# Laying a two-layer kernel's inputs out on the host: direct loads, two more resident weight units, no PE transposes

## The chip, the cores and the metric

The kernel runs on one core of a Trainium2 chip. The metric is the device time of one execution in microseconds, taken as the median of several. Engine names are those of the profile: PE is the matmul engine, PEld its weight load, DVE the vector engine, ACT the scalar engine, POOL is GpSimd, SP the engine that only issues transfers. A name with a q (SPq) is that engine's sequencer. On one core the spread of a kernel is about plus or minus 0.3%. A difference under 2% is called "same" here, even where it is clear of noise. A profile is one execution, so its times scatter as much.

## The reference, cut to what matters

```python
x = x + A(layernorm(x))      # A: memory-augmented recurrent attention, 64 segments of 32 rows
x = x + B(layernorm(x))      # B: sliding, dilated attention, window 8
x = x + A(layernorm(x))      # the same weights again
x = x + B(layernorm(x))
# A, per segment: h = [mem (8 rows), segment (32 rows)]; q,k,v = h Wq, h Wk, h Wv; attention;
# o = . Wo; mem = o[:8] goes into the next segment.  D = 640, 32 heads of 192
```

The memory makes layer A sequential: 64 segments one after the other. The weights of A are 31.5 MB, of which only a part stays on the chip.

## The kernel before

Both passes run at once, as two "lanes" of 40 columns: pass 2 follows pass 1 at a lag of three segments. So 67 steps of A carry 80 columns each, and 69 steps in all finish B. A's weights are cut into 32 units of 0.983 MB. 14 stay in SBUF ("resident"), 18 are loaded again in every step into a ring of four buffers. The sources lie in DRAM in rows of 1280 or 1536 bytes, so that the first load of each ring unit is followed by a copy back to DRAM in rows of 7680 bytes, from which all later steps load.

```python
def unit(self, kind, i):
    ...
    if res:  t_ = self.wres.tile([P, 3840], BF16, ...)
    else:    t_ = self.wring.tile([P, 3840], BF16, name="w_ring")
    if (kind, i) in self.wcopy: nc.sync.dma_start(out=t_[:], in_=self.wcopy[(kind, i)][:])
    else:                       nc.sync.dma_start(out=v, in_=src)          # short rows
    ...
    elif (kind, i) not in self.wcopy:                                      # ring unit, step 0
        self.wcopy[(kind, i)] = self.dram.tile([P, 3840], BF16, ...)
        nc.gpsimd.dma_start(out=self.wcopy[(kind, i)][:], in_=t_[:])
...
def proj_stationary(self, kind, i, t):        # k and q: 30 matmuls of 80 columns
    ...
    nc.tensor.matmul(ps[:, NT*n:NT*(n+1)], lhsT=w[:, c, P*n:P*(n+1)], rhs=hT[:, NT*c:NT*(c+1)], ...)
...
def x_transpose(self, g):                     # every fourth step; y_store likewise
    for c in range(NC):
        nc.tensor.transpose(out=ps[:, c, :], in_=xr[:, P*c:P*(c+1)], identity=self.ident[:])
    nc.scalar.copy(out=xt[:], in_=ps[:])
```

Layer B's weights (wqkv, wo) are loaded at the very start on ACT's queue.

Of the kernel before, what the change touches and what calls it, by code (L numbers as in the profile page):

```python
# [16 lines left out]
DRAM = bass.MemoryType.DRAM  # L17
# [23 lines left out]
N_RES = 14  # L41
# [20 lines left out]
class Kernel:  # L62
    def __init__(self, ctx, tc, A_x, A_mem0, A_Wq, A_Wk, A_Wv, A_Wo, B_wqkv, B_wo, out):
        self.tc = tc
        self.nc = tc.nc
        self.x = A_x[0]
        self.mem0 = A_mem0[0]
        self.out = out[0]
        self.n_seg = A_x.shape[1] // SEG
        self.wsrc = {"k": A_Wk.rearrange("d h e -> d (h e)"), "q": A_Wq.rearrange("d h e -> d (h e)"),  # L70
                     "v": A_Wv.rearrange("d h e -> d (h e)"), "o": A_Wo.rearrange("h e d -> (h e) d")}
        pool = lambda name, bufs, **kw: ctx.enter_context(tc.tile_pool(name=name, bufs=bufs, **kw))
        self.cp = pool("consts", 1)
        self.wres = pool("wres", 1)
        self.wring = pool("wring", RING)
        self.ap2 = pool("act2", 2)
        self.bp = pool("bact", 1)
        self.xp = pool("xio", 1)
        self.ps_big = pool("ps_big", 4, space=PSUM)
        self.ps_one = pool("ps_one", 1, space=PSUM)  # L80
        self.units = {}
        self.wcopy = {}
        self.dram = pool("wdram", 1, space=DRAM)
        self.resident = resident_units()
        self.build_consts(B_wqkv, B_wo)

    def build_consts(self, B_wqkv, B_wo):
        nc, cp = self.nc, self.cp
        nc.scalar.preload_act_table_set("natural_log_exp_and_others")
        ident = cp.tile([P, P], BF16, name="ident")  # L90
        make_identity(nc, ident[:])
        self.ident = ident
# [5 lines left out]
        self.ones = ones  # L98

# [10 lines left out]
        self.maskA = mA  # L110

# [31 lines left out]
        def pers(name, shape, n, dt=BF16, zero=True):  # L143
            ts = []
            for j in range(n):
                t_ = cp.tile(shape, dt, name=f"{name}{j}")
                if zero:
                    nc.vector.memset(t_[:], 0.0)
                ts.append(t_)
            return ts  # L150

        self.hT = pers("hT", [P, NC * NT + 88], 2)
        self.KF = pers("KF", [P, 4 * NT + 48], 2)
        self.Kz = pers("Kz", [P, 4 * NT + 48], 2)
        self.Vt = pers("Vt", [P, 1152], 2)
        self.xin = pers("xin", [P, NC, NX], 3)
        self.h2T = pers("h2T", [P, NC, P], 1)[0]
        self.KB = pers("KB", [P, NBC, P], 1)[0]
        self.VB = pers("VB", [P, BH // 2, 2 * BD + 1], 1)[0]
        nc.vector.memset(self.VB[:, :, BD:BD + 1], 1.0)  # L160
        self.On = pers("On", [P, 3 * P], 1)[0]
        self.YT = pers("YT", [P, NC, P], 1, zero=False)[0]
        self.m0T = pers("m0T", [P, NC, NM], 1, zero=False)[0]
        self.wqkv = cp.tile([P, NC, 3 * D], BF16, name="wqkv_sb")
        nc.scalar.dma_start(out=self.wqkv[:], in_=B_wqkv.rearrange("(c p) n -> p c n", p=P))
        self.wo = cp.tile([P, 2, 3, D], BF16, name="wo_sb")
        nc.vector.memset(self.wo[64:P, :, 2, :], 0.0)
        for par in range(2):
            r0 = par * (D // 2)
            nc.scalar.dma_start(out=self.wo[:, par, 0:2, :], in_=B_wo[r0:r0 + 2 * P, :].rearrange("(m p) n -> p m n", p=P))  # L170
            nc.scalar.dma_start(out=self.wo[0:64, par, 2, :], in_=B_wo[r0 + 2 * P:r0 + D // 2, :])

    def unit(self, kind, i):
        if (kind, i) in self.units:
            return self.units[(kind, i)]
        nc = self.nc
        res = (kind, i) in self.resident
        if kind == "o":
            src = self.wsrc["o"][QE * i:QE * (i + 1), :].rearrange("(m p) d -> p m d", p=P)
        else:  # L180
            src = self.wsrc[kind][:, QE * i:QE * (i + 1)].rearrange("(c p) n -> p c n", p=P)
        if res:
            t_ = self.wres.tile([P, 3840], BF16, name=f"w_{kind}{i}")
        else:
            t_ = self.wring.tile([P, 3840], BF16, name="w_ring")
        v = t_[:].rearrange("p (a b) -> p a b", a=6 if kind == "o" else NC)
        if (kind, i) in self.wcopy:
            nc.sync.dma_start(out=t_[:], in_=self.wcopy[(kind, i)][:])
        else:
            nc.sync.dma_start(out=v, in_=src)  # L190
        if res:
            self.units[(kind, i)] = v
        elif (kind, i) not in self.wcopy:
            self.wcopy[(kind, i)] = self.dram.tile([P, 3840], BF16, name=f"wc_{kind}{i}")
            nc.gpsimd.dma_start(out=self.wcopy[(kind, i)][:], in_=t_[:])
# [7 lines left out]

    def proj_stationary(self, kind, i, t):
# [3 lines left out]
        ps = self.big(f"ps_{kind}")  # L208
        for n in range(6):
            for c in range(NC):  # L210
                nc.tensor.matmul(ps[:, NT * n:NT * (n + 1)], lhsT=w[:, c, P * n:P * (n + 1)], rhs=hT[:, NT * c:NT * (c + 1)],  # L211
# [3 lines left out]
    def a_k(self, i, t):  # L215
# [5 lines left out]
        nc.scalar.copy(out=kf, in_=pv[:, :, 0:3:2, :])  # L221
        nc.scalar.copy(out=kz[0:64, :, 0, :], in_=pv[0:64, :, 1, :])
        nc.scalar.copy(out=kz[64:P, :, 1, :], in_=pv[64:P, :, 1, :])

    def a_q(self, i, t):
        ps = self.proj_stationary("q", i, t)
        qt = self.ap2.tile([P, 6, NT], BF16, name="QT")
        self.nc.vector.tensor_copy(out=qt[:], in_=ps[:, 0:6 * NT].rearrange("p (a n) -> p a n", a=6))  # L228
# [19 lines left out]
    def a_s(self, i):  # L248
# [3 lines left out]
        kf, kz, qt = self.KF[i % 2], self.Kz[i % 2], self.qt  # L252
        for h in range(4):
            pr, j = h // 2, h % 2
            nc.tensor.matmul(sv[:, h, :], lhsT=kf[:, NT * h:NT * h + P], rhs=qt[:, 3 * pr + 2 * j, :], start=True, stop=False)  # L255
            nc.tensor.matmul(sv[:, h, :], lhsT=kz[:, NT * h:NT * h + P], rhs=qt[:, 3 * pr + 1, :], start=False, stop=True)  # L256
        e = self.ap2.tile([P, 4, NT], BF16, name="E")
        nc.scalar.activation(out=e[0:NT], in_=sv[0:NT], func=ACT.Exp, scale=float(DH) ** -0.5)  # L258
        em = self.ap2.tile([P, 4, NT], BF16, name="Em")
        nc.vector.tensor_tensor(out=em[0:NT], in0=e[0:NT], in1=self.maskA[0:NT, :].unsqueeze(1).to_broadcast([NT, 4, NT]), op=ALU.mult)  # L260
        self.em = em

    def a_pv(self, i):
# [3 lines left out]
        dn = self.one("d")  # L267
        nc.tensor.matmul(dn[:, 0:4 * NT], lhsT=self.ones[0:NT, :], rhs=em[0:NT, :, :].rearrange("p h n -> p (h n)"), start=True, stop=True)  # L268
        ops = self.one("o")
        ov = ops[:, 0:6 * NT].rearrange("p (a b n) -> p a b n", a=2, b=3)  # L270
        for pr in range(2):
            for (b, w0, j, st, sp) in [(0, 0, 0, True, True), (1, 128, 0, True, False), (1, 256, 1, False, True), (2, 384, 1, True, True)]:
                nc.tensor.matmul(ov[:, pr, b, :], lhsT=vt[0:NT, 512 * pr + w0:512 * pr + w0 + P], rhs=em[0:NT, 2 * pr + j, :], start=st, stop=sp)  # L273
        r = self.ap2.tile([P, 2, 2, NT], F32, name="R")
        rf = r[:].rearrange("p a b n -> p (a b n)")
        nc.scalar.activation(out=rf, in_=dn[:, 0:4 * NT], func=ACT.Ln)  # L276
        nc.scalar.activation(out=rf, in_=rf, func=ACT.Exp, scale=-1.0)  # L277
        ot = self.ap2.tile([P, 2, 3, NT], BF16, name="OT")
        nc.vector.tensor_tensor(out=ot[:, :, 0:3:2, :], in0=ov[:, :, 0:3:2, :], in1=r[:], op=ALU.mult)  # L279
        nc.vector.tensor_tensor(out=ot[0:64, :, 1, :], in0=ov[0:64, :, 1, :], in1=r[0:64, :, 0, :], op=ALU.mult)  # L280
        nc.vector.tensor_tensor(out=ot[64:P, :, 1, :], in0=ov[64:P, :, 1, :], in1=r[64:P, :, 1, :], op=ALU.mult)
        self.ots[i] = ot

    def a_o(self, i):
# [5 lines left out]
        for m in range(6):  # L290
            for c in range(NC):
                nc.tensor.matmul(self.acc[:, NT * c:NT * (c + 1)], lhsT=w[:, m, P * c:P * (c + 1)], rhs=ot[:, m, :],  # L292
# [5 lines left out]
    def mem_out(self, t):  # L298
# [6 lines left out]
        else:  # L305
            nc.vector.tensor_copy(out=h[:, :, :, 0:NM], in_=a[:, :, :, 0:NM])
# [35 lines left out]
    def b_x1(self, b):  # L342
        nc = self.nc
        a = self.lanes(self.acc[:, 0:NC * NT])
        x1 = self.x1p.tile([P, NC, NX], BF16, name="x1")
        nc.vector.tensor_tensor(out=x1[:].rearrange("p c (l n) -> p c l n", l=2), in0=a[:, :, :, NM:LT],
                                in1=self.xin[b % 3][:].rearrange("p c (l n) -> p c l n", l=2), op=ALU.add)
        self.x1[b] = x1
        self.bsq = self.ln_sq(x1)

    def b_ln(self, b):
        self.bmr = self.ln_small(self.ln_stats(self.x1[b], self.bsq))

    def b_ln_apply(self, b):
        self.ln_big(self.x1[b], self.bmr, self.h2T[:, :, 64 * (b % 2):64 * (b % 2) + NX].rearrange("p c (l n) -> p c l n", l=2))
# [91 lines left out]
    def b_wo(self, b):  # L447
# [7 lines left out]
        x1 = self.x1.pop(b)  # L455
# [8 lines left out]
    def x_load(self, g):  # L464
        xr = self.xp.tile([P, D], BF16, name="xr")
        self.nc.gpsimd.dma_start(out=xr[:], in_=self.x[P * g:P * (g + 1), :])
        self.xr[g] = xr

    def x_transpose(self, g):
        nc = self.nc  # L470
        xr = self.xr.pop(g)
        ps = self.ps_big.tile([P, NC, P], BF16, name="ps_xt", tag="big")
        for c in range(NC):
            nc.tensor.transpose(out=ps[:, c, :], in_=xr[:, P * c:P * (c + 1)], identity=self.ident[:])
        xt = self.xp.tile([P, NC, P], BF16, name="XT4")
        nc.scalar.copy(out=xt[:], in_=ps[:])
        self.xt = xt

    def x_take(self, t):
        o = SEG * (t % 4)  # L480
        self.nc.gpsimd.tensor_copy(out=self.xin[t % 3][:, :, 0:SEG], in_=self.xt[:, :, o:o + SEG])

    def y_store(self, g):
        nc = self.nc
# [164 lines left out]
```

## Time and profile before

| | before |
|---|---|
| time, median of 6 | 3570.51 us (3563.6 to 3579.03) |
| span of the profiled run | 3561.9 us |
| end of step 0 / step 1 | 141.1 / 194.2 us |
| the 64 steps of the middle | 3281.5 us, 51.27 each |
| shortest step | 50.55 us |
| rest (last step, layer B alone, store) | 86.3 us |

A step's end is the start of the DVE copy that carries the memory into the next step; those starts can be read from the timeline of DVE. Below, the "head" is steps 0 and 1, the "middle" the 64 steps after them, a "clean" step one without a wait (50.55 us). An "issue" wait is time in which PE was idle and waited for nothing that the profile shows. In the names of tiles, ps_k, ps_q, ps_v and ps_acc are the projections of A for k, q, v and the output, ps_s, ps_d and ps_o its attention, and a b marks layer B. The lines of the profile stand in the prediction below, with how to read them: a row of the view by stretches gives the stretch, its length, the busy time of each engine with the number of instructions, the granted PE clock (1.00 is full), the DMA share and GB/s.

### The profile page before, as it was taken

The numbers are of one execution on the slowest core, as the hardware profiler recorded it, in microseconds if no ns is written. First come the engines' busy times: TensorE is split into PE (matmuls) and PEld (weight loads), VectorE is DVE, ScalarE is ACT, GpSimd is POOL, SyncE is SP. The second block draws the span as 40 slices with busy tenths as digits, with TensorE's granted clock in tenths as the row PEclk, the third lists the DMA queues.
The fourth block names the chain that finished last, engine by engine and source line by source line (L and its number), as shares of the span: only waits on it lengthen the run. The fifth ranks groups of instructions, "written<-read, shape, count | busy, mean of one in ns | idle before, by whom it ended". The sixth has DMA issues, their size and how long they took to land.

```text
span 3561.9 us, 160052 instructions
## 1 busy us (share of the span) xinstructions
PE 3443.1 (97%) x72592; PEld 3003.7 (84%) x72592; DVE 2063.2 (58%) x5778; ACT 1677.8 (47%) x4723; POOL 67.2 (2%) x201
## 2 busy tenths in 40 slices
PE   4799999999999999999999999999999999999997
PEld 3688888888888888888888888888888888888886
DVE  2355565556565556656665666555656565665564
ACT  1244444444444444444444444544444444445443
POOL 2000000000000000000000000000000000000000
PEclk8799999999999999999999999999999999999998
DMA  9999999999999999999999999999999999999994
GB/s 378 390 340 351 354 348 346 352 349 348 342 358 343 345 349 363 344 341 355 359 348 349 352 362 346 341 353 361 343 343 350 351 349 344 360 351 345 342 363 170
DMA packets 199290, 1235.86 MB, mean 347 GB/s; under 512 B 20424, under 2 KB 42576, under 8 KB 198608
## 3 DMA queue, kind: packets, MB, share of 16 engines
q1 hardware_dynamic: 193088, 1199.39, 89.7%
q0 software_dynamic: 4160, 22.95, 1.6%
q8 instruction: 568, 9.31, 1.0%
q10 hardware_dynamic: 1360, 3.28, 0.2%
q14 instruction: 114, 0.93, 0.1%
HBM read 1205.22 MB, written 20.32 MB: 344 GB/s over the span
## 4 chain that ended last, share of the span: by engine, by line
PE 88%; DMA 7%; issue 4%; POOL 0%; ACT 0%; DVE 0%; SPq 0%; POOLq 0%; ACTq 0%
PE ps_v L239 23%; PE ps_k L211 15%; PE ps_acc L292 15%; PE ps_q L211 15%; PE ps_o L273 4%; PE ps_bv L384 2%; DMA w_ring<-wc_v 2%; PE ps_s L255 2%; PE ps_s L256 2%; PE ps_d L268 2%; DMA w_ring<-wc_o 2%; PE ps_bq L364 2%; PE ps_bk L364 2%; PE ps_by L453 2%; PE ps_bs L408 1%
## 5 line engine op out<-in xcount | busy, mean ns | idle before, releaser
L246 ACT CAST Vt<-ps_v 80x384 bf16<-80x384 f32 x536 | 254.7, 475 | 1287.7 <-PE ps_v L239 1287.7
L239 PEld LDWEIGHTS <-hT 128*128 128x128 bf16 x5360 | 494.4, 99 | 308.7 <-issue 13.9
L279 DVE TENSOR_TENSOR OT<-ps_o,R 128x320 bf16<-128x320 f32 x536 | 263.7, 492 | 774.1 <-ACT R L277 769.9
L211 PEld LDWEIGHTS <-w_ring 128*128 128x128 bf16 x18090 | 687.6, 100 | 18.8 <-DMA w_ring<-in_A_Wq_dram 7.6
L239 PE MATMUL ps_v<-w_v,hT 128*128 128x384 bf16 x3350 | 606.7, 328 | 11.0 <-DMA w_v<-in_A_Wv_dram 9.0
L292 PE MATMUL ps_acc<-OT,w_ring 128*128 128x80 bf16 x12060 | 503.9, 203 | 15.4 <-DMA w_ring<-in_A_Wo_dram 9.0
L228 DVE CAST QT<-ps_q 128x480 bf16<-128x480 f32 x536 | 352.5, 658 | 233.2 <-PE ps_q L211 224.7
L292 PEld LDWEIGHTS <-w_ring 128*128 128x128 bf16 x12060 | 461.0, 100 | 18.8 <-DMA w_ring<-in_A_Wo_dram 9.9
L244 DVE CAST Vt<-ps_v 80x384 bf16<-80x384 f32 x536 | 296.0, 552 | 250.4 <-PE ps_v L239 242.3
L211 PE MATMUL ps_k<-hT,w_ring 128*128 128x80 bf16 x10050 | 418.4, 202 | 5.5 <-DMA w_ring<-in_A_Wk_dram 2.7
L239 PE MATMUL ps_v<-w_ring,hT 128*128 128x384 bf16 x2010 | 363.3, 328 | 10.8 <-DMA w_ring<-wc_v 5.8
L211 PE MATMUL ps_q<-hT,w_ring 128*128 128x80 bf16 x8040 | 336.0, 203 | 10.8 <-DMA w_ring<-in_A_Wq_dram 7.2
L211 PE MATMUL ps_q<-hT,w_q 128*128 128x80 bf16 x8040 | 333.7, 202 | 4.9 <-DMA w_q<-in_A_Wq_dram 3.5
L211 PEld LDWEIGHTS <-w_q 128*128 128x128 bf16 x8040 | 306.1, 100 | 3.9 <-DMA w_q<-in_A_Wq_dram 3.9
L221 ACT CAST KF<-ps_k 128x320 bf16<-128x320 f32 x536 | 227.4, 424 | 134.5 <-PE ps_k L211 134.5
L276 ACT ACTIVATE R<-ps_d 128x320 f32<-128x320 f32 x536 | 232.4, 434 | 103.8 <-PE ps_d L268 103.8
L273 PEld LDWEIGHTS <-Vt 80*128 80x128 bf16 x4288 | 221.2, 98 | 51.3 <-issue 3.4
L277 ACT ACTIVATE R<-R 128x320 f32<-128x320 f32 x536 | 251.8, 470 | 17.0
L211 PE MATMUL ps_k<-hT,w_k 128*128 128x80 bf16 x6030 | 250.0, 202 | 0.6 <-DMA w_k<-in_A_Wk_dram 0.4
L273 PE MATMUL ps_o<-Em,Vt 80*128 80x80 bf16 x4288 | 241.6, 200 | 2.3 <-issue 1.6
L258 ACT ACTIVATE E<-ps_s 80x320 bf16<-80x320 f32 x536 | 227.6, 425 | 24.5 <-PE ps_s L256 24.3
L211 PEld LDWEIGHTS <-w_k 128*128 128x128 bf16 x6030 | 229.3, 100 | 0.9 <-DMA w_k<-in_A_Wk_dram 0.6
(110 smaller groups left out, 4330.3 us busy)
## 6 DMA issues: line engine op xcount, KB each, us to landing
w_ring<-wc_o SPq DMA_DIRECT2D x396, 960.0 KB, 7.3
w_ring<-wc_k SPq DMA_DIRECT2D x330, 960.0 KB, 7.3
w_ring<-wc_q SPq DMA_DIRECT2D x264, 960.0 KB, 7.0
w_ring<-wc_v SPq DMA_DIRECT2D x198, 960.0 KB, 7.0
w_ring<-in_A_Wo_dram SPq DMA_DIRECT2D x6, 960.0 KB, 17.0
wc_o<-w_ring POOLq DMA_DIRECT2D x6, 960.0 KB, 8.1
w_ring<-in_A_Wk_dram SPq DMA_DIRECT2D x5, 960.0 KB, 17.1
w_v<-in_A_Wv_dram SPq DMA_DIRECT2D x5, 960.0 KB, 16.5
```

The costliest lines, as they stand in the source:

```text
L211: nc.tensor.matmul(ps[:, NT * n:NT * (n + 1)], lhsT=w[:, c, P * n:P * (n + 1)], rhs=hT[:, NT * c:NT * (c + 1)], start=(c == 0), stop=(c == ...
L221: nc.scalar.copy(out=kf, in_=pv[:, :, 0:3:2, :])
L228: self.nc.vector.tensor_copy(out=qt[:], in_=ps[:, 0:6 * NT].rearrange("p (a n) -> p a n", a=6))
L239: nc.tensor.matmul(ps[:, 0:384], lhsT=hT[:, NT * c:NT * c + P], rhs=w[:, c, 384 * pr:384 * (pr + 1)], start=(c == 0), stop=(c == NC - 1))
L244: nc.vector.tensor_copy(out=dst, in_=src)
L246: nc.scalar.copy(out=dst, in_=src)
L258: nc.scalar.activation(out=e[0:NT], in_=sv[0:NT], func=ACT.Exp, scale=float(DH) ** -0.5)
L273: nc.tensor.matmul(ov[:, pr, b, :], lhsT=vt[0:NT, 512 * pr + w0:512 * pr + w0 + P], rhs=em[0:NT, 2 * pr + j, :], start=st, stop=sp)
L276: nc.scalar.activation(out=rf, in_=dn[:, 0:4 * NT], func=ACT.Ln)
L277: nc.scalar.activation(out=rf, in_=rf, func=ACT.Exp, scale=-1.0)
L279: nc.vector.tensor_tensor(out=ot[:, :, 0:3:2, :], in0=ov[:, :, 0:3:2, :], in1=r[:], op=ALU.mult)
L292: nc.tensor.matmul(self.acc[:, NT * c:NT * (c + 1)], lhsT=w[:, m, P * c:P * (c + 1)], rhs=ot[:, m, :], start=(i == 0 and m == 0 and c == 0 ...
```

## The change

The intent is to let the host do all the layout. Each unit, x, the memory and layer B's weights come in the form in which SBUF wants them; the write-back copies, the transposes through PE and their ACT copies go; SBUF that the transposes and the software DMA's scratch held goes to two more resident units. The diff, cut:

```diff
-N_RES = 14
+N_RES = 16
 def unit(self, kind, i):
-    if (kind, i) in self.wcopy: nc.sync.dma_start(out=t_[:], in_=self.wcopy[(kind, i)][:])
-    else:                       nc.sync.dma_start(out=v, in_=src)
+    self.nc.sync.dma_start(out=t_[:], in_=self.wA[self.place[(kind, i)]])     # rows of 7680 bytes
-    elif (kind, i) not in self.wcopy: ... nc.gpsimd.dma_start(out=self.wcopy[(kind, i)][:], in_=t_[:])
 def x_load(self, g):
-    self.nc.gpsimd.dma_start(out=xr[:], in_=self.x[P*g:P*(g+1), :])           # then x_transpose
+    self.nc.scalar.dma_start(out=self.xt[g][:]..., in_=self.x[g])             # already transposed
 def y_store(self, g):
-    ... 5 transposes, an ACT copy, a DMA from GpSimd
+    self.nc.scalar.dma_start(out=self.out[g], in_=self.YT[:]...)
 def build_consts(self):
-    nc.scalar.dma_start(out=self.wqkv[:], ...)          # and wo: at the start, ACT's queue
 def step(self, t):
+    if t == 0: self.load_b_weights()                    # SP's queue, behind step 0's units
-nc = _bacc.Bacc(...)
+nc = _bacc.Bacc(..., dynamic_dma_scratch_size=256)
```

The column slices that the change also brings in ("span_of") always cover both lanes, so no matmul changes.

## The prediction

> **What bounds the kernel now.** I read the page's busy shares first, then cut the run into stages with the view of busy time by stretches, then the waits of the matmul engine in the long middle stage, then the transfers. The page alone would say "PE 97% busy, done"; the question is what the other 3% are.
>
> ```profile
> PE 3443.1 (97%) x72592; PEld 3003.7 (84%) x72592; DVE 2063.2 (58%) x5778; ACT 1677.8 (47%) x4723; POOL 67.2 (2%) x201
> ...
> PEclk8799999999999999999999999999999999999998
> DMA  9999999999999999999999999999999999999994
> ...
> q1 hardware_dynamic: 193088, 1199.39, 89.7%
> ```
>
> Two resources are near full for the whole span: PE and the 16 DMA engines. The kernel runs 69 steps. The small copy that carries the memory into the next step (vector engine, ps_acc to hT) closes each step, so its start times are the step boundaries: 141.1 us for step 0, 194.2 for step 1, 3475.7 for the last one. I cut there, and added two single steps:
>
> ```profile
> core 0: us, PE busy (x) PEld busy (x) DVE busy (x) ACT busy (x) POOL busy (x), PEclk, DMA share, GB/s
> 0.00:30.00 30.00, 1.94 (x20) 1.60 (x21) 6.51 (x24) 1.98 (x2) 20.57 (x93) 1.00 0.98 341
> 30.00:141.10 111.10, 69.99 (x946) 54.56 (x946) 23.81 (x61) 21.63 (x60) 8.61 (x17) 0.72 1.04 396
> 141.10:194.20 53.10, 50.71 (x1004) 43.86 (x1004) 25.55 (x66) 22.08 (x62) 0.38 (x1) 0.94 0.97 380
> 194.20:3475.70 3281.50, 3254.57 (x69341) 2848.69 (x69338) 1964.92 (x5503) 1598.97 (x4510) 37.14 (x89) 1.00 0.93 350
> 3475.70:3562.00 86.30, 65.92 (x1294) 55.02 (x1290) 42.37 (x127) 33.13 (x89) 0.54 (x1) 0.86 0.44 165
> 811.57:862.12 50.55, 50.55 (x1087) 44.33 (x1084) 30.64 (x86) 24.69 (x70) 0.00 (x0) 1.00 0.94 351
> 2706.59:2759.61 53.02, 51.33 (x1092) 44.79 (x1089) 30.76 (x86) 25.28 (x71) 1.36 (x3) 1.00 0.92 342
> ```
>
> The head (to 194.2) is DMA-bound: share 0.97 to 1.04 while PE is 63% busy at clock 0.72. The middle is PE-bound: the clean step of 50.55 us has no PE gap. As a check I summed the chain of a step: 16 projections of 1.07, eight ps_acc groups of 1.08, eight ps_v of 1.62, the small groups and layer B give 50.5. So 50.55 is the floor of a step, and 64 steps are 64 x 50.55 = 3235.2; the stage took 3281.5. The excess of 46.3 us is all that a change in loads can win there. Its waits:
>
> ```profile
> PE ps_v L239 <- DMA w_ring<-wc_v: 5.8, 10, 1.4
> PE ps_q L211 <- issue: 4.0, 5, 1.4
> PE ps_acc L292 <- issue: 3.0, 6, 1.0
> PE ps_acc L292 <- DMA w_ring<-wc_o: 2.3, 4, 1.0
> PE ps_v L239 <- issue: 2.0, 4, 0.9
> PE ps_s L256 <- issue: 1.9, 4, 0.9
> ```
>
> DMA waits: 8.1 us in 14. "issue" waits, all rows of that answer: 15.6 us in 30. Waits for ACT and DVE and one PE row: 2.6 in 4. Transposes through PE (29 groups of five, 0.28 us each in the chain): 8.1. That leaves about 11 us, which I spread over the 48 interruptions as 0.235 us each (pipeline drain and refill).
>
> **What the Trainium skill says.** "TensorE: Matmul & The Clock Gate", section "Back-to-back issue gap": N/2.4 + 2.5 ns when warm. For N = 80 that is 35.8 ns, 30 of them 1.075 us; the trace's groups of 30 take 1.07, so the floor really is the array. The same page, Part 1: after some 3.4 us of idling the clock halves; the trace agrees, 30 matmuls take 2.18 us in step 0. "DMA: Bandwidth & Descriptors", section "Issuing engines are not separate DMA queues": queues share the same 16 engines, so moving a load to another queue adds no rate. The trace agrees: 396 GB/s with three queues in step 0, 380 in step 1 with nearly one. "HBM Reference", Specifications, says about 425 GB/s for a lone core; the trace never holds that, so I use 380.
>
> **The change part by part.** The arrays are laid out on the host. Several things follow.
>
> 1. Write-back copies gone. Before, 18 ring units (128 x 3840 x 2 bytes = 0.983 MB) were loaded with 1280 to 1536-byte rows and written back to DRAM once: 17.7 MB. All 32 units are 31.5 MB; layer B's weights 3.3 MB lay at the very start. Total about 52.7 MB; at 380 to 396 GB/s 133 to 139 us, which is the 141.1 at which step 0 ended. After: 31.5 MB and 0.16 MB of x, 31.6/380 = 83.2 us, plus 3 us until the first byte flows, plus about 2 us of hole: the ring lets 8 units (21 us) go before the first k must be consumed, and that waits for GpSimd, which builds masks until about 22 us in the trace of before, with x taken somewhere in between (I put k0 at 21 to 22). The last unit lands at 88.2.
>
> 2. Layer B's weights now follow step 0 on the same queue: 2.46 + 0.98 = 3.44 MB, 9.05 us, then step 1's k0 (2.6 us) lands: 88.2 + 9.05 + 2.6 = 99.9. The last output projection and the memory copy take 3 us of these 11.7 and hide. Step 1 is a step without layer B's second half (ps_bs 0.88, ps_bo 0.40, ps_bt 0.17, ps_by 0.88) and without the 0.88 of ps_bq behind its boundary: 50.55 - 2.33 - 0.88 = 47.3, plus 3.2 us of cold clock in its first groups. The second boundary falls at 150.5 instead of 194.2: **43.7 us won**. This is the largest part.
>
> 3. Transposes gone: 29 x 0.28 = **8.1 us** from the middle, all on PE's path, since it has no slack there. The ACT copies (0.69 us, 32 times) were off the path.
>
> 4. Two more resident units: 16 ring loads a step instead of 18. At 370 to 380 GB/s they need 42 us of 50.55; DMA share falls from 0.93 to about 0.84, and ring and resident units now alternate strictly, where before two ring units met in a row. I take the DMA waits (8.1 + 14 x 0.235 = 11.4 us) to fall to 1. The issue waits (15.6 + 30 x 0.235 = 22.7) strike in the middle of a group of matmuls, where no semaphore is; the instruction queue moved 9.31 MB, which is about 64 bytes for each of PE's 145,000 instructions, so I read them as late instruction fetches on the same DMA engines. A less loaded DMA should cut some: I choose 14. The rest 3.5 to 3. Gain 10.4 + 8.7 + 0.5 = **19.6**.
>
> 5. The tail: the last store loses its PE transpose, ACT copy and GpSimd issue (from 3554.6 to 3556.9) and keeps its landing: **2.8**. The rest of the tail is a chain of small layer B operations, unchanged.
>
> 6. The slices of "span_of" always cover everything, so no matmul shrinks. x loads and y stores are issued by ACT now, 16 each, some 0.5 us, in the place of the 0.69 us copies: nothing.
>
> Sum: 43.7 + 8.1 + 19.6 + 2.8 = 74.2; span 3561.9 - 74.2 = 3487.7.
>
> **Rivals.** (a) *Issue waits do not care about DMA load.* They arise from round-robin, not from queue length; 22.7 us stay. For it: share 0.84 is still busy. Against: nothing in this profile. Then 3496 to 3498, on the edge of 2%. (b) *All waits are the DMA's.* Steps at 50.55 to 50.6 throughout: 3471. For it: 12 or so clean steps exist already. (c) *The head is worth less.* If x is taken only after all masks, k0 starts at 26 to 27 and 4 to 5 us of DMA time are lost; a rate of 360 costs 5 more: 3497. If instead contiguous rows run at 400 and more, 3481. (d) *The load was hidden anyway*, so only transposes and tail count: about 3550. Against: PE stands 41 us of the 111 in step 0, and DMA is over 1.0 busy there. (e) *ACT becomes late*, as an x load there waits for GpSimd or a store for YT and holds up the exponentials. Both producers finish tens of us earlier in the program, so at most 32 x 0.5 = 16 us: 3504. No resource becomes a new bound that would make it slower.
>
> **Range and chances.** The profiled run of before was its fastest (3563.6, span 3561.9); the median of six is 3570.5. The ratio 3487.7/3561.9 = 0.979 puts the median at 3496; if waits shrink, their spread shrinks too, and 3487.7 + 1.7 + 2 = 3491. I take 3491, range 3465 to 3515 from (b) at the low end and (a), (c), (e) partly together at the high end. 2% lies at 3499, close: faster 0.63, within 2% 0.36, slower 0.01.
>
> **What would show it.** The step boundary of step 0 near 91 us and of step 1 near 150; in step 0 the DMA share still about 1; k0 of step 1 waiting some 9 us behind layer B's weights. In the middle, DMA share near 0.84, no PE wait for ring units above 1 us in total, steps of 50.55 where 50.83 stood, issue waits around 9 us. I am wrong if step 0 ends after 100, if the middle exceeds 3262 us, or if waits for ACT or DVE appear in PE's list.

## The result, and the profile after

| | before | after | difference | predicted |
|---|---|---|---|---|
| time, median | 3570.0 us (16 runs) | 3477.46 us (8 runs, 3473.74 to 3486.04) | | 3491 |
| span of the profiled run | 3561.9 | 3476.9 | -85.0 | -74.2 |
| end of step 0 | 141.1 | 87.6 | -53.5 | 91 |
| end of step 1 | 194.2 | 146.1 | -48.1 | -43.7 |
| 64 middle steps | 3281.5 | 3248.2 | -33.3 | -27.7 |
| rest | 86.3 | 82.7 | -3.6 | -2.8 |

The ratio is 0.9742, with a 95% interval of 0.9728 to 0.9756: faster by 2.6%. A ratio is the mean time of one kernel's fast runs over that of the other's of the same rounds, so not quite the ratio of the medians quoted.

The page of the changed kernel answers to the first lines of the prediction:

```profile
PE 3408.9 (98%) x72427; PEld 2981.2 (86%) x72427; DVE 2058.4 (59%) x5777; ACT 1658.3 (48%) x4691; POOL 40.4 (1%) x150
...
PEclk9999999999999999999999999999999999999998
DMA  9989888888988898898888888888988988898894
...
q1 hardware_dynamic: 156960, 1073.06, 86.0%
```

PE has 165 matmuls fewer, exactly the transposes (33 groups of five, 30 of them in the middle), and the DMA engines carry 126 MB less on SP's queue. The view by stretches of the changed kernel, cut at its own step ends and twice more in step 0:

```profile
core 0: us, PE busy (x) PEld busy (x) DVE busy (x) ACT busy (x) POOL busy (x), PEclk, DMA share, GB/s
0.00:20.00 20.00, 0.78 (x10) 0.73 (x11) 5.82 (x24) 1.28 (x1) 15.93 (x80) 1.00 0.92 366
20.00:30.00 10.00, 7.89 (x127) 7.04 (x127) 2.89 (x8) 2.75 (x9) 2.37 (x10) 1.00 0.64 241
30.00:87.60 57.60, 44.83 (x825) 36.43 (x821) 20.92 (x52) 18.65 (x52) 0.00 (x0) 0.94 1.01 417
87.60:146.10 58.50, 50.37 (x1002) 43.86 (x1003) 25.55 (x65) 22.09 (x62) 0.38 (x1) 0.88 0.96 360
146.10:3394.30 3248.20, 3239.22 (x69191) 2838.25 (x69188) 1960.78 (x5502) 1581.05 (x4480) 21.70 (x60) 1.00 0.88 314
3394.30:3477.00 82.70, 65.80 (x1291) 54.92 (x1287) 42.40 (x127) 32.44 (x88) 0.00 (x0) 0.88 0.43 151
```

Three things are to be seen. Step 0 is still bound by the DMA engines (share 1.01) but at 417 GB/s and with 31.6 MB to move. Between 20 and 30 us there is a hole: 241 GB/s, share 0.64. And in the middle PE is idle for 9.0 us where it was 26.9 before. What is left of the waits there is in this list of the changed kernel's middle (us in total, times, longest); no row of it names a DMA:

```profile
PE ps_q L204 <- issue: 2.3, 4, 1.0
PE ps_v L233 <- issue: 1.6, 2, 1.2
PE ps_acc L288 <- issue: 1.3, 3, 0.6
```

All "issue" rows of that answer sum to 8.1 us in 16 waits; of the 64 middle steps 45 now take 50.55 to 50.61 us, against 14 before, where 30 steps had a group of transposes as well. The boundary between steps 0 and 1 in the timeline of the changed kernel (start, length, engine, line, operation):

```profile
66.68 0.33 SPq L180 DMA_DIRECT2D w_o<-in_wA_dram  x1
69.01 0.33 SPq L169 DMA_DIRECT2D wqkv_sb<-in_wqkv_dram  x1
71.35 0.33 SPq L170 DMA_DIRECT2D wo_sb<-in_wo_dram  x1
73.73 24.55 SPq L180 DMA_DIRECT2D w_ring<-in_wA_dram  x5
...
95.73 2.18 PE L204 MATMUL ps_k<-hT,w_ring 128*128 128x80 bf16 x30 [8.16 <-DMA w_ring<-in_wA_dram]
```

SP issues step 0's last unit, then layer B's 3.44 MB, then step 1's first ring unit. The queue serves them in that order, so PE waits 8.16 us for its first k, and starts it at a cold clock: the 30 matmuls take 2.18 us, where the same group takes 1.24 in run 8 below, in which it does not wait.

### The profile page after: what moved, and what is told of

Its sections match the earlier page's. It is cut to its first block, busy times and chain, and to the rows that moved or that the text cites.

```text
span 3476.9 us, 159281 instructions
## 1 busy us (share of the span) xinstructions
PE 3408.9 (98%) x72427; PEld 2981.2 (86%) x72427; DVE 2058.4 (59%) x5777; ACT 1658.3 (48%) x4691; POOL 40.4 (1%) x150
## 3 DMA queue, kind: packets, MB, share of 16 engines
q8 instruction: 566, 9.27, 1.0%
## 4 chain that ended last, share of the span: by engine, by line
PE 97%; DMA 2%; issue 0%; POOL 0%; DVE 0%; ACT 0%; POOLq 0%; SPq 0%; ACTq 0%
PE ps_v L233 25%; PE ps_k L204 17%; PE ps_q L204 16%; PE ps_acc L288 16%; PE ps_o L269 4%; PE ps_bv L381 3%; PE ps_s L250 2%; PE ps_s L251 2%; PE ps_d L264 2%; PE ps_by L450 2%; PE ps_bq L361 2%; PE ps_bs L405 2%; PE ps_bk L361 2%; PE ps_st L315 1%; DMA w_ring<-in_wA_dram 1%; PE ps_bo L426 1%
## 5 line engine op out<-in xcount | busy, mean ns | idle before, releaser
L233 PE MATMUL ps_v<-w_v,hT 128*128 128x384 bf16 x4690 | 842.2, 327 | 5.1 <-DMA w_v<-in_wA_dram 3.9
L204 PE MATMUL ps_k<-hT,w_ring 128*128 128x80 bf16 x14070 | 584.1, 202 | 10.7 <-DMA w_ring<-in_wA_dram 8.2
L204 PE MATMUL ps_q<-hT,w_q 128*128 128x80 bf16 x14070 | 585.0, 202 | 5.2 <-DMA w_q<-in_wA_dram 2.6
L288 PE MATMUL ps_acc<-OT,w_ring 128*128 128x80 bf16 x14070 | 583.2, 202 | 5.7 <-DMA w_ring<-in_wA_dram 4.5
L204 PEld LDWEIGHTS <-w_q 128*128 128x128 bf16 x14070 | 536.4, 100 | 6.2 <-issue 3.2
L215 ACT CAST KF<-ps_k 128x320 bf16<-128x320 f32 x536 | 226.8, 423 | 135.1 <-PE ps_k L204 134.9
L250 PE MATMUL ps_s<-QT,KF 128*128 128x80 bf16 x2144 | 222.5, 200 | 0.9 <-issue 0.9
L251 PE MATMUL ps_s<-QT,Kz 128*128 128x80 bf16 x2144 | 222.4, 201 | 0.0
L255 DVE TENSOR_TENSOR Em<-E,maskA 80x320 bf16<-80x320 bf16 x536 | 170.1, 317 | 40.6 <-ACT E L253 34.1
L250 PEld LDWEIGHTS <-KF 128*128 128x128 bf16 x2144 | 171.7, 98 | 14.5 <-issue 1.3
## 6 DMA issues: line engine op xcount, KB each, us to landing
w_o<-in_wA_dram SPq DMA_DIRECT2D x1, 960.0 KB, 18.6
```

The lines of the kernel that those rows point to most:

```text
L204: nc.tensor.matmul(ps[:, NT * n + c0:NT * n + c1], lhsT=w[:, c, P * n:P * (n + 1)], rhs=hT[:, NT * c + c0:NT * c + c1], start=(c == 0), st ...
L233: nc.tensor.matmul(ps[:, 0:384], lhsT=hT[:, NT * c:NT * c + P], rhs=w[:, c, 384 * pr:384 * (pr + 1)], start=(c == 0), stop=(c == NC - 1))
L250: nc.tensor.matmul(sv[:, h, cs], lhsT=kf[:, NT * h:NT * h + P], rhs=qt[:, 3 * pr + 2 * j, cs], start=True, stop=False)
L251: nc.tensor.matmul(sv[:, h, cs], lhsT=kz[:, NT * h:NT * h + P], rhs=qt[:, 3 * pr + 1, cs], start=False, stop=True)
L288: nc.tensor.matmul(self.acc[:, NT * c + self.cs.start:NT * c + self.cs.stop], lhsT=w[:, m, P * c:P * (c + 1)], rhs=ot[:, m, self.cs], star ...
```

## The experiments

The theory: the head gained by bytes that no longer move, the middle by the lighter load on the DMA engines (no waits for ring units, fewer late instruction fetches) plus the transposes' own time. The rivals: the middle gained from transposes, copies and queues and not from the residents; the issue waits have nothing to do with the DMA; the head gained by long rows or by the order of the loads. Twelve kernels ran. Those of runs 1, 2, 4 and 5 are "same" as the kernel before by the 2% rule, the others faster. Single rows of the view by stretches are quoted without their heading; their columns are those above.

**1. The changed kernel with 14 resident units.**

```diff
-N_RES = 16
+N_RES = 14
```

> The changed kernel with 14 resident units instead of 16, all else kept: 18 ring loads a step. Theory (both the waits for ring units and the issue waits come from the load on the DMA engines): DMA share of the middle back to about 0.93, waits for ring units back to 6 to 10 us and issue waits from 8 to about 14 us in the 64 middle steps, which become 3260 to 3275 us instead of 3248; time about 3495 to 3505. Rival (transposes, copies and queues made the middle faster, the residents did not): waits stay, middle 3250, time about 3480.

Measured: 3511.24 us (ratio to before 0.9841). End of step 1 at 148.8, and the middle:

```profile
148.80:3433.80 3285.00, 3249.45 (x69189) 2841.02 (x69186) 1963.04 (x5502) 1579.26 (x4480) 21.69 (x60) 1.00 0.93 349
```

In these two profiles the two units are worth 36.8 us of the middle (3285.0 - 3248.2), more than the theory's 12 to 27. The largest rows of its waits:

```profile
PE ps_acc L288 <- issue: 9.1, 13, 1.4
PE ps_v L233 <- DMA w_ring<-in_wA_dram: 6.1, 14, 1.1
```

Ring waits came back as expected (7.7 us in 19), the issue waits to 26.9 us in 44, more than in the kernel before (15.6 in 30) at the same 0.93. The direction decides against the rival. That 18 loads seem to hurt more here than there is within what single profiles scatter: the profiled execution of this kernel was its slowest of four (3517.33 us, 6.1 over the median), that of the kernel before was 6.4 us faster than its median, and with 16 units at 314 GB/s the issue waits of single profiles lie between 5.9 (run 2) and 13.7 us (run 10).

**2. The kernel before with 16 resident units, nothing else.** Its own transposes, copies and load order stay; the software-DMA scratch is cut to 1024 so that the tiles fit.

```diff
-N_RES = 14
+N_RES = 16
-num_devices=1)
+num_devices=1, dynamic_dma_scratch_size=1024)
```

> The kernel before with only the residents changed, 16 instead of 14, for which its software-DMA scratch is cut to 1024; copies, transposes and order of loads stay. Theory: the middle drops from 3281 to about 3257 (transposes stay, waits for ring units gone, issue waits about halved), step 0 loses two of 18 write-back copies (2 MB, 5 us); time about 3540. Rival (residents worth little alone): 3565 or more.

Measured: 3527.51 us, ratio 0.9886. Step 0 ends at 136.2 (4.9 earlier), step 1 at 185.8, and the middle:

```profile
185.80:3439.00 3253.20, 3246.48 (x69340) 2846.70 (x69336) 1964.19 (x5502) 1596.26 (x4510) 37.60 (x89) 1.00 0.88 314
```

The middle lost 28.3 us with the 8.4 us of transposes still in it (30 groups of 0.28), no wait for a ring unit is left, and issue waits are 5.9 us. So in these profiles this part alone gives 28.3 of the change's 33.3 us in the middle, and 38.1 of the 85.0 us of the span. The time, too, is better than the theory's 3540. Runs 1 and 2 together are a table of two by two: the layout without the residents gives 1.6% (0.9841), the residents without the layout 1.1% (0.9886), both 2.6% (0.9742).

**3. Half of the bytes in the ring.** From step 1 on each ring load brings half a unit, and the matmuls read that half twice. The result is wrong on purpose (relative error 0.022); the number and size of the matmuls are unchanged.

```diff
+if (kind, i) in self.seen:
+    self.nc.sync.dma_start(out=t_[:, 0:1920], in_=src[:, 0:1920])
+    return Half(t_, 640 if kind == "o" else QE)      # slices taken modulo 1920 columns
```

> The changed kernel with ring loads of half the bytes from step 1 on (wrong result on purpose; the same number of matmuls of the same sizes). DMA share of the middle about 0.45. Theory (issue waits are instruction fetches that are late because the DMA engines are busy): issue waits in the middle fall from 8.1 to under 2.5 us and the 64 steps take 3235 to 3239; time about 3463. Rival (issue waits have nothing to do with DMA load): they stay at 6 to 10 us, middle about 3246, time about 3473.

Measured: 3463.36 us (3462.23 to 3464.23). The middle:

```profile
144.08:3379.63 3235.55, 3235.55 (x69190) 2837.50 (x69187) 1962.06 (x5503) 1578.27 (x4480) 21.67 (x60) 1.00 0.53 160
```

The DMA share is 0.53 (about 0.45 was expected). PE is busy for 3235.55 of 3235.55 us: not one wait, each of 64 steps at 50.55 or 50.56, and the spread of the four runs is 2 us where the changed kernel's is 12. The rival falls: issue waits go with the DMA load. That they are instruction fetches stays an argument (the instruction queue moved 9.27 MB, 64 bytes for each PE instruction, on the same engines), not something a run isolates.

**4. The write-back copies put back, on GpSimd.**

```diff
+if not res and (kind, i) not in self.copied:
+    self.copied[(kind, i)] = self.dram.tile([P, 3840], BF16, ...)
+    self.nc.gpsimd.dma_start(out=self.copied[(kind, i)][:], in_=t_[:])
```

> The changed kernel with the write-back of each ring unit to DRAM in step 0 put back (16 copies, 15.7 MB, results unused). Theory (step 0 is bound by the bytes that the DMA engines move, in either direction): step 0 ends at about 125 us instead of 87.6, time about 3513. Rival (writes run beside reads for nothing, the gain of the head came from long rows or from the order of loads): step 0 ends at 88 to 95, time about 3480.

Measured: 3564.19 us, step 0 ends at 155.2, and the DMA share in it falls to 0.80. Both sides missed. The timeline of POOL shows a fault of the experiment:

```profile
46.93 0.54 POOL L185 DMA_DIRECT2D wc_k<-w_ring  x1 [9.35 <-issue]
57.59 0.53 POOL L185 DMA_DIRECT2D wc_o<-w_ring  x1 [10.12 <-issue]
```

One copy starts every ten microseconds, about the 10 us that one takes to land, and SP stands waiting for them (78.3 us in the k copies alone). The change had cut the software queue's scratch to 256 bytes; it seems to hold one such copy (with the 1024 of run 2 copies started as little as 2.7 us apart, and POOL waited only for the loads). The change can afford that only as it no longer issues any DMA from GpSimd. Nothing follows for the bytes.

**5. The same copies, issued by ACT.**

```diff
-    self.nc.gpsimd.dma_start(out=self.copied[(kind, i)][:], in_=t_[:])
+    self.nc.scalar.dma_start(out=self.copied[(kind, i)][:], in_=t_[:])
```

> The write-back of 16 ring units in step 0 again, now issued by ACT instead of GpSimd, as the software queue with its 256 bytes of scratch let one copy go at a time (step 0 ended at 155 with the DMA share at 0.80). Theory (step 0 is bound by bytes moved): 31.6 + 15.7 MB at about 400 GB/s, step 0 ends at 120 to 128 us at a DMA share near 1, time 3510 to 3520. Rival (the copies hold the ring's buffers and so cost more than their bytes): step 0 ends at 135 or later with a DMA share well under 1.

Measured: 3512.83 us; step 0 ends at 120.0, step 1 at 177.8.

```profile
30.00:120.00 90.00, 56.64 (x815) 44.61 (x811) 20.92 (x52) 18.59 (x51) 0.00 (x0) 0.76 1.02 425
```

The theory holds: the engines are full, at 425 GB/s counted over both directions, and the head is longer by 31.7 us at the end of step 1 (177.8 - 146.1). The 15.7 MB at 425 GB/s would be 37 us; a part of the copies fell between 20 and 30 us, where the engines now moved 356 GB/s instead of 241. In the middle nothing changes (50.76 us a step).

**6. Short rows in all loads.** Each unit lies in DRAM as the old sources were cut, and is loaded so in every step.

```diff
-self.nc.sync.dma_start(out=t_[:], in_=self.wA[n])
+self.nc.sync.dma_start(out=v, in_=self.wA[n].rearrange("(a p b) -> p a b", p=P, ...))
```

> The changed kernel with each weight unit stored in DRAM as the old sources were cut, 5 x 128 rows of 1536 bytes or 6 x 128 of 1280, in place of 128 rows of 7680 bytes; all loads of all steps read so. Theory (step 0 gained by fewer bytes, rows give the small rest): rate in step 0 390 to 400 instead of 417 GB/s, its end at 89 to 94; in the middle SP's issues become longer and the DMA share rises to 0.88 to 0.92, waits for ring units return in part, time 3490 to 3510. Rival (rows were the larger part of the head's gain): step 0 ends at 105 or later, and the middle becomes DMA-bound, over 3600.

Measured: 3484.83 us (ratio 0.9768). Step 0 and the middle:

```profile
30.00:93.70 63.70, 43.75 (x816) 36.13 (x812) 20.93 (x52) 18.31 (x51) 0.00 (x0) 0.97 1.06 374
152.60:3402.40 3249.80, 3239.68 (x69189) 2838.11 (x69185) 1961.63 (x5502) 1580.53 (x4480) 21.71 (x60) 1.00 0.95 314
```

The rate in step 0 falls from 417 to 374 GB/s and the end of step 1 moves from 146.1 to 152.6: rows are worth about 6.4 us of the head (run 7, whose head is that of the changed kernel, ended step 1 at 144.6, so 1.6 us is scatter). In the middle they cost nothing, against the expectation: the share is 0.95, yet no wait names a DMA, and issue waits are 8.6 us in 17. So issue waits go with the bytes and not with the busy share: 314 GB/s here and in the changed kernel, 349 with 14 residents (run 3 kept the number of loads and halved the bytes). It suggests that with 16 residents the kernel of before could have done without its write-back copies; that was not run.

**7. The transposes put back** (31 groups of five, with an ACT copy each, on data nobody reads).

```diff
+if i == 2 and (t % 4 == 3 or t % 4 == 1) and 3 <= t < self.n_seg:
+    self.dummy_transpose()
```

> The changed kernel with 31 groups of five PE transposes and an ACT copy each put back at the places of the old ones (of data that nobody reads). Theory: PE has no slack in the middle, so each group costs its 0.28 us: the steps that have one take 50.83 instead of 50.55, the middle is 8 us longer, time about 3485. Rival (they fit into gaps that PE has anyway, or they also unsettle the order of buffers): under 3 us, or over 12.

Measured: 3483.31 us (ratio 0.9748), 5.9 us over the changed kernel's median; the middle is 3257.8, 9.6 us longer, and the steps with a group take 50.83 or 50.84 us where nothing else happens. In the steps of the trace the 0.28 us per group stand on PE's path in full, as the theory says; the times alone could not show it, as the ratios differ by 0.0006 and have intervals of 0.2%.

**8. Layer B's weights in step 1, after its third group of units.**

```diff
-if t == 0: self.load_b_weights()           # end of step 0
+if t == 1 and i == 2: self.load_b_weights()
```

> The changed kernel with layer B's weights loaded in step 1 after the third group of units instead of at the end of step 0. Theory: the first k of step 1 stood 8.2 us behind these 3.44 MB; now it starts at about 88 us, and the end of step 1 comes at 139 to 141 instead of 146.2; time about 3471. Rival (the DMA engines bound step 1 too, so the bytes only move): the wait returns later in step 1, its end stays at 145 or later.

Measured: 3474.01 us; step 1 ends at 143.3. Only 2.8 us are won, of which 1.6 can be scatter (run 7): the wait of 8.2 us before the first k is gone, and most of it comes back a few units later, where the chain passes through 15.5 us of ring loads from 92 us on. Nearer to the rival: the bytes only move.

**9. Layer B's weights at the very start, on ACT's queue, as before.**

> The changed kernel with layer B's weights loaded at the very start on ACT's queue, as in the kernel before. Theory (the head counts bytes): step 0 ends 8 us later, at about 95, the first k of step 1 does not wait, the end of step 1 is 144 to 147, time 3475 to 3480. Rival (their place in the queue is part of the gain): end of step 1 at 150 or later.

Measured: 3471.27 us (ratio 0.9713); step 0 ends at 90.5, step 1 at 138.3, 7.8 us ahead of the changed kernel. Better than the theory, which let step 0 pay for the bytes in full. The reason is the hole:

```profile
20.00:30.00 10.00, 5.74 (x73) 5.04 (x73) 2.69 (x9) 1.50 (x5) 2.05 (x9) 1.00 1.02 420
30.00:87.00 57.00, 44.92 (x846) 36.75 (x845) 20.20 (x49) 18.92 (x53) 0.00 (x0) 0.97 1.01 418
```

In the changed kernel these ten microseconds moved 241 GB/s, since the ring was full and its first unit not yet consumed (SP waited 15.3 us for that k); layer B's weights need no ring and fill the hole. So the change gave back some 8 us of this head by moving them; in the times it is 6 us by the medians, and the intervals of the two ratios (0.9691 to 0.9736, 0.9728 to 0.9756) still touch.

**10. Weights late and x taken early.** As 8, with layer B's masks built on GpSimd after the first x is taken.

```diff
 self.prologue()
+self.build_masks()          # taken out of build_consts
```

> Layer B's weights late, and layer B's masks built after the first x is taken, so that GpSimd takes x at about 5 us instead of 18.5. Theory: the first k starts at 9 to 11 us instead of 22.1, the hole of the DMA engines at 20 to 30 us (241 GB/s) closes, step 0 ends at 82 to 84, and time is about 4 us under the one with only the weights late. Rival (step 0 is bound by the rate alone, the hole is filled later): same time within 1 us.

Measured: 3469.15 us (ratio 0.9730, not apart from run 8's 0.9727). The first k starts at 12.1 us instead of 22.1 (9 to 11 was expected), step 0 ends at 82.2, 5.6 us earlier than in run 8, and the hole is closed (417 GB/s); step 1 ends at 139.1. The profiled run, the slowest of the four, had 13.7 us of issue waits, which hid the gain in that execution. That it shows in the time is not shown.

**11. and 12. One lane where one is empty.** In the first and last three steps of A one lane carries nothing. Run 11 adds to run 10, run 12 to run 9:

```diff
-self.l0, self.l1 = 0, 2
+self.l0, self.l1 = (0 if t < self.n_seg else 1), (1 if t < LAG else 2)
```

> The same, and in the three first and three last steps of layer A, in which one of the two lanes carries nothing, the matmuls that move lane columns move 40 instead of 80. Estimate: [...]some 9 us a step; steps 0 and 1 are bound by DMA and keep their length, steps 2, 64, 65, 66 shorten by 6 to 9 us each as far as 16 ring loads (38 to 41 us) allow; time 3435 to 3445, and results still correct.

> The version that the runs point to: layer B's weights at the very start on ACT's queue (they fill the hole of the DMA engines at 20 to 30 us), masks as in the changed kernel, and 40 columns instead of 80 in the six steps with one empty lane. Step 0 ends at 90 to 91; step 1 is then bound by its 16 ring loads (37.7 us at 417 GB/s), its end at 129 to 132 instead of 134.5 of the run with the weights late; steps 2, 64, 65, 66 as there (issue waits keep them near 47 to 48 us); time 3444 to 3449. Rival: the wait for ring units moves into step 2 and nothing is won over 3451.

Measured: 3450.95 us (ratio 0.9673) and 3451.93 us (0.9674), both correct and both faster than either kernel; their order is open. The gain is smaller than estimated: in run 11 steps 2, 64 and 65 are 2 to 3.5 us shorter than a clean step. Step 2 of run 11:

```profile
134.50:182.40 47.90, 42.23 (x1085) 35.25 (x1081) 25.11 (x86) 19.60 (x70) 0.32 (x1) 1.00 0.91 333
```

The 40-column matmuls start 25 ns apart (30 in 0.76 us; 30 of 80 columns take 1.07), but PE then stands 5.5 us of the step in issue waits. That it goes through its instructions faster than they come is a reading that no run isolates. In run 12 step 1 ended at 134.9 instead of 129 to 132: it was bound by the DMA engines (share 1.01 at 405 GB/s; 18.6% of its chain is ring loads, 8.2% issue).

## Why the prediction was right

The time came out at 3477.46, inside 3465 to 3515, and faster by over 2%, as given at 0.63. The five terms:

- *Part 1, copies and head.* Right in mechanism and shown by run 5. The rate was mis-sized: 380 GB/s was the mean of step 1 before, whose loads already had long rows but did not keep the engines full throughout (fortieths of it lie between 208 and 451 GB/s); step 0 with long rows and a full queue ran at 417 (short rows: 374, run 6). 31.6/417 is 75.8 us instead of 83.2. Two smaller errors ran against it: the hole cost 4.2 us (10 x (1 - 241/417)) instead of 2, and the first 20 us ran at 366. Step 0 ended at 87.6 instead of 91, closer than the rate alone would have brought it, as these errors partly cancelled; k0 began at 22.1, as placed.
- *Part 2, layer B's weights.* The wait was there, 8.2 us for some 9, and step 1 lasted 58.5 us for 59.5. What the prediction did not see is that this move is a loss: in their old place the weights fill the hole (run 9, 7.8 us).
- *Part 3, transposes.* 8.1 us predicted; the middle lost 150 matmuls, which are 30 groups and not 29, so 8.4 us, and run 7 shows 0.28 for each.
- *Part 4, residents.* Right in mechanism, and the term that was mis-sized most: 19.6 us predicted. The profiles give 24.9 (33.3 less 8.4 for the transposes), 28.3 (run 2) and 36.8 (run 1), and scatter as said under run 1. The ratios, which rest on all fast runs, agree better: 0.0099 between run 1 and the changed kernel is 35 us, less 2.7 in the head 33; 0.0114 of run 2 is 41 us, less 8.4 in the head 32; the change's own 0.0258 is 92 us, less 48.1 in the head, 3.6 in the rest and 8.4 for transposes 32. So the residents are worth about 32 us (an estimate, good to some 5 to 7 us), and the change gained more in the middle than the 33.3 us of the table, as the profiled run of the kernel before was a fast one. In the profile, DMA waits fell to 0 instead of 1; issue waits to 8.1 + 16 x 0.235 = 11.9 instead of 14. The excess over 64 clean steps is 13.0 us instead of 18. The DMA share came out at 0.88, not 0.84.
- *Part 5, tail.* 3.6 us for 2.8 (the stretch that the prediction names, 3554.6 to 3556.9, is 2.3 long): the store from ACT also lands sooner (2.9 us from the last vector operation to the end, against 7.4).

Of the rivals, (a), issue waits blind to the DMA load, fell by run 3, and (b) was the right reading of the cause, though not all waits went with two units. Of (c), the late x did not come (GpSimd took it at 18.5 us, among the masks), and the rate of 400 and more for long rows did. (d) and (e) showed no sign; no wait for ACT or DVE is in PE's list of the middle.

Two readings of the prediction need a word. It sets 2.18 us for 30 matmuls at the cold clock beside 1.07; these are not alike, as the first group after a wait takes 1.24 at full clock, and groups that follow without one take 2.00 cold and 1.07 warm (before and after 97.9 us of the changed kernel, and run 8). And the section that it cites for N/2.4 + 2.5 ns gives this for an isolated matmul and says that it under-counts in a stream with weight loads; here every matmul has its weight load (72427 of each), and 35.7 ns apart the formula held.

The terms of the head don't add up from the runs: 31.7 us for 16 copies, 6.4 for rows, 8.4 for two residents more in the kernel before, less 7.8 for layer B's weights make 38.7 of 48.1. The earlier first k (22.1 against 32.2 us) was not tried by itself in the kernel before. A shift of the same size (22.1 to 12.1 us, run 10 against run 8) was worth 5.6 us at the end of step 0, where it closed a hole; the kernel before had no such hole (share 0.98 up to 30 us). The rest stays open.

## What to carry to other kernels

When two resources are both near full, look for a step without any wait: its length is the floor, and what all steps together take beyond it is what a lighter load can win at most (here 46.3 us, of which the transposes were 8.4; with half of the ring's bytes the floor was reached). Size a term from the times of many executions, not from one profile of each kernel. A load that needs no ring buffer belongs where the ring holds up the queue, which can be earlier than where it is needed. And a load cut from 93% of the DMA engines to 88% was worth more than the waits that name a DMA, as PE's "issue" waits went with it.

## What the Trainium skill lacked or had wrong

- No page tells that PE can stand in issue waits because the DMA engines are loaded: 15.6 and 26.9 us at 350 and 349 GB/s (the kernel before, run 1), 8.1 at 314 (the changed kernel), none at 160 (run 3); these are single profiles, and others at 314 GB/s lie between 5.9 and 13.7. If these waits are late instruction fetches, which is not shown, it belongs to "Runtime: NRT & Kernel Launch", section "Instruction fetch mechanics".
- "DMA: Bandwidth & Descriptors", section "Specifications", gives 512 bytes as the least transfer for line rate. Rows of 1280 to 1536 bytes ran at 374 GB/s and rows of 7680 at 417 in the same step of the same kernel.
- "TensorE: Matmul & The Clock Gate", Part 4, gives about 275 ns for a transpose in a kernel's context. Here one took 219 ns from start to end, and in a stream that is not what it costs: five took 0.28 us of PE's path, 56 ns each.
- No page says what a small software-DMA scratch does: with 256 bytes, copies of 128 rows from GpSimd started one every 10 us (run 4).
